# Sums over tokens with both signs of phi in one weight: 65 moving columns for 129, and due times by refinement

## The chip, the cores and the metric

The kernel runs on one core of a Trainium2 chip. The metric is the device time of one execution in microseconds; lower is better. Eight runs of the kernel before gave a median of 390.5 us, between 389.41 and 391.68. All profile numbers come from one profiled execution of it.

The engines are TensorE (PE in the profile; its weight loads are PEld), VectorE (DVE), ScalarE (ACT), GpSimd (POOL) and the SyncE queue (SP), which issues nearly all DMA transfers. Each runs its own queue of instructions in order and waits on semaphores for the others.

## The reference

The input is 2048 tokens of 512 features, in bf16. Two layers follow one another, each of a linear attention with 32 heads of 16 features (Hedgehog) and a gated MLP of 1376 hidden features. Cut to what matters:

```python
pq = einsum("bhsd,hdf->bhsf", q, w_phi);  pk = einsum("bhsd,hdf->bhsf", k, w_phi)
phi_q = concatenate([softmax(pq), softmax(-pq)], -1)       # 32 features per head
phi_k = concatenate([softmax(pk), softmax(-pk)], -1)
kv  = einsum("bhsf,bhsd->bhfd", phi_k, v)                  # sum over all tokens
z   = einsum("bhsf->bhf", phi_k)                           # sum over all tokens
o   = einsum("bhqf,bhfd->bhqd", phi_q, kv) / (einsum("bhqf,bhf->bhq", phi_q, z)[..., None] + 1e-6)
x = x + o @ wo                                             # of layernorm(x)
x = x + ((relu(g) * u) @ W_down)                           # g, u = layernorm(x) @ W_gate, W_up
```

For every head a 32 x 17 table is needed: 16 positive and 16 negative features of the keys, times 16 value features and a one for z. Only blocks of equal head are wanted; a matmul over 128 keys' features and 128 value features also computes the products of unequal heads.

## The kernel before

**Tiles.** The 2048 tokens are 16 tiles of 128. A layer has these stages per tile:

- *Norm and keys.* Statistics and normalisation on DVE (L610, L611, L621, two small ACT steps L616 and L618), a transpose by DMA (`turn`, L598, tile `xnTA`), four matmuls of 512 columns for the key features (L641; `w_phi` is folded into the weight beforehand) and four for the values (L647). ACT takes exp of the keys with both signs into `ek` (L644), DVE sums 16 features at a time (L652), ACT makes the reciprocal by log and exp (L655, L657), and `phi` (L661) multiplies, on DVE or POOL, half a tile in an instruction, into `phiK`. The values are copied from PSUM to `vext`, which has one extra column of ones.
- *Sums over tokens* (`kvz`, L675 to L686). Eight matmuls per tile: one for each block b of eight heads and each sign s, weight `ph[:, s, b*128:(b+1)*128]` (128 tokens x 128 features), moving `vext` of 129 columns (128 value features and the ones). They add up over all 16 tiles of a layer in three PSUM banks of pool `q`: groups 0 to 2, 3 to 5, 6 and 7.
- *R* (`Keys.build`, L688). When the last sum is in, DVE multiplies each bank by the head mask `Mf` into the bf16 tile `R`, laid out as [128 features, 8 groups, 18, 8 heads]: 16 value features, z, and a column of the mask itself (written once, L551). The masked products are zeros where heads differ, so all of R is written each time.
- *Queries* (L715, exp with both signs on ACT into `Eq`, L719), per chunk of four tiles.
- *Attention* (`attend`, L725). For each tile eight matmuls of 144 columns (`erq`, L733) with `Eq` as weight and a group of R as moving operand, in three PSUM buffers of pool `q` (3, 3 and 2 matmuls). Each buffer is emptied by two copies through `evac`: the numerators into `N`, the denominators into `DS`. Then DVE makes `m`, `den`, `rden`, `w`, `pr` and `o` (L749 to L761), `o` is transposed (by DMA, or by TensorE and a copy for the first two tiles), projected (L765) and added to X (L769).
- *MLP* (`mlp`, L774) in blocks of 1, 1, 2, 4, 4, 2, 2 tiles (the second layer ends in 1, 1): statistics and centring on DVE, transpose, gate and up matmuls (L829; the last 96 hidden features apart, L805), relu on ACT (L833), a copy of the up projection by `evac`, their product on DVE (L837), down matmuls (L862) and the residual (L869). In layer 0 each tile goes on to the norm and keys of layer 1.

**PSUM.** Eight banks: three in pool `q` (sums, erq), five in pool `b` (everything else), L459.

**The order of the work.** The program is not written in its final order. Each operation is an `Op` with an engine, a cost, a due time, the operations it depends on and the buffers that it takes and uses. `plan` (L76) is a list scheduler: at each step it picks, on the engine that can start first, the ready operation with the lowest due time, by costs written into the file (`mm`, `act`, `dve` and so on), and emits it. The instructions of each engine run in the order so found. Before, the due times come from `DUE`, a table of 2112 stored numbers, one per operation, which replaces the due times given in the code (`arrange`, L160). A second stored table, `PLACE` (301 characters, 117 of them "1"), decides for every copy out of PSUM and every phi product whether it stays on the engine that the code names first or changes to its other one: ACT or DVE for copies, POOL or DVE for phi. By default copies go to ACT (the code names DVE for some of the first ones), and phi follows `PHI0` in layer 0 and is DVE for most of layer 1.

**Idle fillers.** Until the first sum, matmuls of zeros (L557) fill gaps of TensorE.

Of the kernel before, what the change touches and what calls it, by code (L numbers as in the profile page):

```python
# [8 lines left out]
P = 128  # L9
# [10 lines left out]
GV = P + 1  # L20
# [139 lines left out]
def arrange(ops):  # L160
# [8 lines left out]
    assert len(ops) == len(DUE)  # L169
    for n, o in enumerate(ops):  # L170
        o.n, o.due = n, DUE[n]
        o.follow += {taker[b] for b in o.uses} - set(o.deps) - set(o.follow)
        for d in o.deps:
            d.then.append(o)
        for d in o.follow:
            d.behind.append(o)
    return plan(ops)
# [26 lines left out]
DVE0 = (85, 170)  # L204
STATS = (592, 692)
# [11 lines left out]
class K:  # L217
# [8 lines left out]
PLACE = (  # L226
    "0000010000001001000100000001010000000000101100111000110100010000100001001000000000100100101011010000"
    "1000000000111101000110100111010010111011010100100110101011010000101011001110000110000000111000000101"
    "1100101010101000101000110000000100000100110010110011011101000010011110010100010111101011111011011010"
    "1"  # L230
)
# [3 lines left out]

DUE = (
    7238437, 6462738, 6444986, 6386567, 5992333, 6335033, 6406961, 6303369, 5712831, 6413612, 6092682, 6414331,
    7434675, 6620170, 4674366, 7071562, 5773774, 7071571, 7071548, 7071565, 5376048, 6430379, 5994524, 5038937,  # L240
    5154841, 6509440, 6825368, 6847621, 6377520, 5995707, 6404704, 6443663, 6844264, 5995988, 6959386, 6784947,
    6825065, 6420713, 6382495, 5410283, 6400005, 6216969, 7068818, 6425562, 6371338, 6325356, 5116853, 6509939,
    6325403, 6399345, 6420906, 6420903, 6403761, 5854885, 5527927, 6112383, 6040357, 6246638, 6429204, 6120059,
    6425464, 5996011, 5410344, 5937857, 5997209, 6629949, 6159020, 5837281, 6159017, 5812166, 6376057, 6112054,
    5527770, 5778741, 5859984, 6246016, 5780700, 6191478, 5995462, 6415371, 6420993, 5937862, 6218721, 6366108,
    6398876, 6355933, 6040362, 6353076, 6692318, 6246832, 6301941, 6333817, 6305472, 6420324, 6246635, 6282608,
    6010072, 6010132, 5937718, 5517502, 5527720, 5962872, 6417645, 6375834, 6115594, 6417622, 6376951, 6040201,
    6418805, 6367897, 6418065, 6246853, 6246635, 6280551, 6416172, 6413450, 5812833, 5734989, 5527730, 6415701,
    6589688, 6660152, 6259055, 6293340, 6418857, 6193613, 6400771, 6242577, 5594853, 5897821, 6418101, 6246214,
    6414310, 6418410, 6417781, 6293326, 6418213, 6337803, 6493628, 5823924, 6281803, 6385607, 6385616, 6414319,  # L250
    6392870, 6399165, 6376822, 6423098, 6382355, 6246148, 6189671, 6413294, 5970487, 6354744, 6354741, 6148511,
    6557117, 6415725, 7222162, 6412246, 6420372, 6418246, 6414304, 6330448, 6400107, 6407313, 6121354, 6246632,
    6247421, 6281496, 6418264, 6416104, 6292977, 6417603, 6446115, 6428567, 5823973, 6417942, 6323224, 6435617,
    6413175, 6372016, 6395620, 6424638, 6323105, 6245911, 6245802, 6350052, 6399800, 6339292, 6104846, 6199296,
    6400901, 6500288, 6429150, 6504253, 6415373, 5944333, 5942659, 6414885, 6419661, 6437686, 6424884, 6421739,
# [163 lines left out]
def kernel(  # L419
# [209 lines left out]
    class Keys:  # L629
# [57 lines left out]

        def build(self, due):  # L688
            made = []
            for k in range(3):  # L690
                ng = 3 if k < 2 else 2

                def num(k=k, ng=ng):
# [278 lines left out]
```

The softmax here doesn't subtract the row's maximum and nothing guards it: scores larger than these inputs give would overflow.

## Time and profile before

| | |
|---|---|
| time, median of 8 runs | 390.5 us |
| time of the profiled execution | 390.68 us |
| its span, first to last instruction | 388.9 us |
| granted TensorE clock | 1.00 |
| TensorE busy | 381.6 us (98%) |
| VectorE busy | 309.2 us (80%) |
| ScalarE busy | 217.7 us (56%) |
| GpSimd busy | 43.5 us (11%) |
| sums: 256 matmuls of 129 columns (L678) | 19.4 us busy |
| erq: 256 matmuls of 144 columns (L733) | 26.8 us busy |
| copies of the up projection | 46 on ACT (26.1 us), 37 on DVE (25.1 us) |
| phi products | 39 on POOL (42.8 us), 25 on DVE (16.7 us) |
| copies of N: ACT / DVE | 63 / 33 |
| value copies: ACT / DVE | 21 / 11 |

A group's row has its line, engine, operation, tiles and count, then busy time, the mean duration of one in ns, and the idle time of the engine just before. Matmuls are pipelined: a matmul of 129 columns lasts 220 ns from start to end, but the next one starts long before that end, so busy time of a run of matmuls is much less than count times duration, and a short gap between matmuls can hide in the duration of the one before. A wait's row reads: who waited, for whom, us in all, times, longest. A window's row gives busy time and count of each engine, then clock, DMA share and GB/s.

### The profile page before, as it was taken

How to read it: one execution, taken by the hardware profiler on the slowest of the kernel's cores; microseconds unless marked ns; L12 is line 12 of the kernel's file. 1: busy time of each engine (PE TensorE's matmuls, PEld its weight loads, DVE VectorE, ACT ScalarE, POOL GpSimd, SP SyncE). 2: the span in 40 equal slices, each digit the busy share in tenths (PEclk: the TensorE clock that was granted, in tenths of full speed). 3: DMA queues.
4: the chain of work that ended last, by engine and by line, in shares of the span. 5: the costliest groups of instructions: out<-in, count | busy, mean ns of one | idle time of the engine just before them, and what ended most of it. 6: DMA issues, size and time to landing. Idle time of an engine off the chain costs nothing.

```text
span 388.9 us, 7655 instructions
## 1 busy us (share of the span) xinstructions
PE 381.6 (98%) x2833; PEld 231.6 (60%) x2833; DVE 309.2 (80%) x785; ACT 217.7 (56%) x569; POOL 43.5 (11%) x45
## 2 busy tenths in 40 slices
PE   8999998999999999999999999999999999999996
PEld 4544565967654554454767655578765545547674
DVE  6999988999999985479767486799998999455243
ACT  6999979744556545134665668976425520443111
POOL 0344630000200400012220122000000000000000
DMA  8479840122322221102201000023233122201110
GB/s 247 103 165 196 189 136 1 37 55 50 78 59 42 56 53 30 27 16 54 43 0 15 14 15 0 2 33 64 56 70 81 37 50 66 54 7 29 56 35 29
DMA packets 60871, 22.84 MB, mean 59 GB/s; under 512 B 52673, under 2 KB 59809, under 8 KB 60833
## 3 DMA queue, kind: packets, MB, share of 16 engines
q1 hardware_dynamic: 60416, 21.95, 26.2%
q8 instruction: 22, 0.36, 0.4%
q10 hardware_dynamic: 416, 0.39, 0.3%
q14 instruction: 17, 0.13, 0.1%
HBM read 7.91 MB, written 2.10 MB: 26 GB/s over the span
## 4 chain that ended last, share of the span: by engine, by line
PE 82%; DVE 7%; ACT 5%; DMA 3%; issue 1%; DVEq 0%; ACTq 0%
PE b L829 34%; PE b L862 19%; PE b L765 6%; PE b L641 5%; PE b L647 5%; PE b L715 4%; PE q L678 3%; PE b L805 3%; PE q L733 2%; ACT Eq L719 2%; DMA xnTA<-xn 2%; ACT ek L644 1%; DMA xnTB<-xn 1%; DVE pr L758 1%; DVE X L769 1%; DVE bstB L610 1%
## 5 line engine op out<-in xcount | busy, mean ns | idle before, releaser
L829 PE MATMUL b<-xnTB,wgu 128*128 128x128 bf16 (+2 forms) x1200 | 150.8, 279 | 0.0
L829 PEld LDWEIGHTS <-wgu 128*128 128x128 bf16 x1200 | 97.8, 98 | 42.8
L862 PE MATMUL b<-wd,hT 128*128 128x512 bf16 (+2 forms) x363 | 83.4, 373 | 0.0
L833 ACT ACTIVATE gu<-b 128x512 bf16<-128x512 f32 (+1 forms) x83 | 48.1, 582 | 48.2 <-PE b L829 45.4
L661 POOL TENSOR_TENSOR phiK<-ek,sk 128x512 bf16<-128x512 bf16 x39 | 42.8, 1116 | 193.5 <-ACT sk L657 144.7
L862 PEld LDWEIGHTS <-hT 128*128 128x128 bf16 (+1 forms) x363 | 34.8, 98 | 34.9 <-DVE hT L837 0.3
L837 DVE TENSOR_TENSOR hT<-gu 128x512 bf16<-128x512 bf16 (+1 forms) x83 | 33.7, 407 | 18.5 <-ACT gu L563 16.9
L644 ACT ACTIVATE ek<-b 128x512 bf16<-128x512 f32 x64 | 35.9, 598 | 17.1 <-PE b L641 17.0
L652 DVE TENSOR_REDUCE sk<-ek 128x64 f32<-128x1024 bf16 x32 | 38.6, 1209 | 8.1 <-ACT ek L644 8.0
L563 ACT CAST gu<-b 128x512 bf16<-128x512 f32 (+1 forms) x46 | 26.1, 566 | 31.7 <-PE b L829 31.7
L719 ACT ACTIVATE Eq<-b 128x512 bf16<-128x512 f32 x64 | 35.3, 623 | 4.7 <-PE b L715 4.5
L564 DVE CAST gu<-b 128x512 bf16<-128x512 f32 (+1 forms) x37 | 25.1, 677 | 13.2 <-PE b L829 13.0
L869 DVE SCALAR_TENSOR_TENSOR X<-b,rsB,X 128x512 bf16<-128x512 f32 (+1 forms) x33 | 23.4, 726 | 15.1 <-PE b L862 15.0
L641 PE MATMUL b<-Wk,xnTA 128*128 128x512 bf16 x128 | 32.9, 379 | 0.5 <-DMA xnTA<-xn 0.5
L647 PE MATMUL b<-wv,xnTA 128*128 128x512 bf16 x128 | 32.4, 379 | 0.6 <-DMA xnTA<-xn 0.6
L563 ACT CAST N<-q 128x384 bf16<-128x384 f32 (+1 forms) x63 | 28.0, 461 | 8.3 <-DVE pr L758 3.2
L765 PE MATMUL b<-wo,oT 128*128 128x512 bf16 x128 | 32.5, 379 | 0.0
L715 PE MATMUL b<-xnTA,Wq 128*128 128x512 bf16 x128 | 31.2, 379 | 0.0
L733 PE MATMUL q<-R,Eq 128*128 128x144 bf16 x256 | 26.8, 226 | 1.0 <-ACT N L563 0.5
L733 PEld LDWEIGHTS <-Eq 128*128 128x128 bf16 x256 | 19.9, 98 | 11.3 <-issue 1.4
L610 DVE BATCH_NORM_STATS2 bstA<-X 128x6 f32<-128x512 bf16 x32 | 21.2, 682 | 3.0 <-DMA X<-in_A_x_dram 2.9
L769 DVE TENSOR_TENSOR X<-X,b 128x512 bf16<-128x512 bf16 x32 | 21.6, 677 | 1.6 <-PE b L765 1.5
(71 smaller groups left out, 397.3 us busy)
## 6 DMA issues: line engine op xcount, KB each, us to landing
out_dram<-X SPq DMA_DIRECT2D x15, 128.0 KB, 1.7
X<-in_A_x_dram SPq DMA_DIRECT2D x6, 256.0 KB, 3.3
wgu<-in_B_W_gate_dram SPq DMA_DIRECT2D x4, 344.0 KB, 4.3
wgu<-in_B_W_up_dram SPq DMA_DIRECT2D x4, 344.0 KB, 5.2
wd<-in_B_W_down_dram SPq DMA_DIRECT2D x5, 256.0 KB, 4.8
wv<-in_A_wqkv_dram SPq DMA_DIRECT2D x2, 256.0 KB, 4.2
wo<-in_A_wo_dram SPq DMA_DIRECT2D x4, 128.0 KB, 3.6
oT<-o SPq DMA_TRANSPOSE x28, 2.4
```

What stands on the lines that cost most here:

```text
L563: both = {"ACT": ("ACT", act(cols), lambda: nc.scalar.copy(out=out_(), in_=in_()), False), "DVE": ("DVE", dve(cols), lambda: nc.vector.ten ...
L641: k = op("PE", mm(4, 512), due, lambda: [nc.tensor.matmul(kp.t[:], lhsT=xnTA[c][:, b, cols], rhs=Wk2[:, b, :], start=(b == 0), stop=(b == ...
L644: e = [op("ACT", act(512), due, lambda s=s: nc.scalar.activation(out=ek.t[:, s, :], in_=kp.t[:], func=AF.Exp, scale=1.0 - 2.0 * s), [k], [ ...
L647: v = op("PE", mm(4, 512), due_v, lambda: [nc.tensor.matmul(vp.t[:], lhsT=xnTA[c][:, b, cols], rhs=wv[:, b, :], start=(b == 0), stop=(b == ...
L661: e.tensor_tensor(out=ph.t[:].rearrange("p s (h f) -> p (s h) f", f=DH)[:, lo:lo + n], in0=ek.t[:].rearrange("p s (h f) -> p (s h) f", f=D ...
L715: q = op("PE", mm(4, 512), due(c, b), lambda b=b, qp=qp: [nc.tensor.matmul(qp.t[:], lhsT=Wq2[:, m, b * P:(b + 1) * P], rhs=xnTA[c][:, m, : ...
L719: done.append(op("ACT", act(512), due(c, b), lambda b=b, s=s, qp=qp: nc.scalar.activation(out=Eq[c][:, b, s, :], in_=qp.t[:], func=AF.Exp, ...
L733: pe.append(op("PE", mm(len(groups), GE), due, lambda ps=ps, groups=groups: [nc.tensor.matmul(ps.t[:, n * GE:(n + 1) * GE], lhsT=Eq[c][:, ...
L765: a = op("PE", mm(4, 512), due + 3, lambda: [nc.tensor.matmul(yp.t[:], lhsT=oT.t[:, b, :], rhs=wo[:, b, :], start=(b == 0), stop=(b == NB ...
L829: nc.tensor.matmul(ps.t[:, q * W:(q + 1) * W], lhsT=wgu[:, s, b, g * P:(g + 1) * P], rhs=xT.t[:, b, 0:W], start=(b == 0), stop=(b == NB - 1))
L833: nc.scalar.activation(out=gu.t[:, 0, 0:cols], in_=gp.t[:, 0:cols], func=AF.Relu)
L862: nc.tensor.matmul(yp.t[:, 0:c1 - c0], lhsT=h.t[:m, f * W + i * P:f * W + (i + 1) * P], rhs=wd[:m, f, c0:c1], start=(f == 0), stop=(f == N ...
```

## The change

Four things change together.

1. *The sums.* `ek` and `phiK` are laid out as [8 groups of four heads, 2 signs, 64 features]. A group's weight is its four heads with both signs, again 128 columns; the moving operand is the values of these four heads and a one, 65 columns (`vext` is laid out as 8 groups of 65, padded to 66). There are still eight matmuls per tile. The eight results of 65 columns fit in two banks: even groups in one, odd ones in the other. The planner books 8 x 40 ns for them (`SUMS`).
2. *R.* A result now has the positive features of its four heads in partitions 0 to 63 and the negative ones in 64 to 127. `erq` is unchanged, so R keeps its layout, and `build` moves halves between partitions: for each bank and sign one masked product over 64 partitions x 256 elements and one for z, eight pairs in all over two layers for six. The parts of R that are never written are zeroed once at the start (`c_r0`).
3. *PSUM.* Pool `q` has two banks for three, pool `b` six for five. `erq` uses pool `q` too: the three buffers of a tile now take turns in two banks.
4. *The order.* `DUE` goes. The due times given in the code are refined: `plan` runs, `back` goes through the plan from its end and gives each operation the latest time at which it could end in a reversed schedule as its due time, and this is repeated ten times; the due times of the plan with the earliest end are kept. `PLACE` is empty, so every copy and every phi product stays on the engine that the code names.

The diff, without the stored tables:

```diff
-GV = P + 1
+NG = 2 * NB
+HG = HB // 2
+GQ = P // 2
+GV = GQ + 1
...
+def back(ops):
+    left = {o: len(o.then) + len(o.behind) for o in ops}
+    ready = dict.fromkeys(ops, 0.0)
+    clock = dict.fromkeys(HOP, 0.0)
+    open_ = {e: [o for o in ops if o.eng == e and not left[o]] for e in HOP}
+    for _ in ops:
+        best = None
+        for e, cand in open_.items():
+            if cand:
+                at = [(max(clock[e], ready[o] + o.end - o.start - o.spent), o) for o in cand]
+                first = min(t for t, o in at)
+                if best is None or first < best[0]:
+                    best = first, max((o for t, o in at if t <= first + 1), key=lambda o: (o.start, o.n))
+        t, o = best
+        clock[o.eng] = t + o.spent
+        o.due = -clock[o.eng]
...
-def arrange(ops):
+def refine(ops, rounds):
...
-    assert len(ops) == len(DUE)
     for n, o in enumerate(ops):
-        o.n, o.due = n, DUE[n]
+        o.n = n
...
+    best = None
+    for k in range(rounds):
+        dues = [o.due for o in ops]
+        span = max(o.end for o in plan(ops))
+        if best is None or span < best[0]:
+            best = span, dues
+        back(ops)
+    for o, due in zip(ops, best[1]):
+        o.due = due
     return plan(ops)
...
+SUMS = (8 * 40, 8 * 40 + 170)
...
-PLACE = (
...
+ROUNDS = 10
+PLACE = ""
...
-    p_q, p_b = psum("q", 3), psum("b", 5)
+    p_q, p_b = psum("q", 2), psum("b", 6)
-    p_ek, p_phi = pool("ek", 4, [2, D]), pool("phiK", 4, [2, D])
+    p_ek, p_phi = pool("ek", 4, [NG, 2, GQ]), pool("phiK", 4, [NG, 2, GQ])
-    p_v = pool("vext", 5, [NB, GV])
+    p_v = pool("vext", 5, [NG, GV + 1])
...
+    c_r0 = op("DVE", dve(1152, 4), 15000, lambda: nc.vector.memset(R[:], 0.0), follow=[c_z], name="R0", port=True)
...
-                out=ek.t[:, s, :], in_=kp.t[:], func=AF.Exp, scale=1.0 - 2.0 * s), [k], [ek] if s == 0 else [],
+                out=ek.t[:, :, s, :], in_=kp.t[:].rearrange("p (g e) -> p g e", e=GQ), func=AF.Exp, scale=1.0 - 2.0 * s), [k], [ek] if s == 0 else [],
...
             def kvz():
-                for g in range(2 * NB):
-                    b, s = g // 2, g % 2
-                    nc.tensor.matmul(self.bufs[g // 3].t[:, (g % 3) * GV:(g % 3 + 1) * GV],
-                                     lhsT=ph.t[:, s, b * P:(b + 1) * P], rhs=vx.t[:, b, :],
-                                     start=(self.n == 0 and g % 3 == 0), stop=(self.n == T - 1),
+                for g in range(NG):
+                    b, k = g // 2, g % 2
+                    nc.tensor.matmul(self.bufs[k].t[:, b * GV:(b + 1) * GV],
+                                     lhsT=ph.t[:, g, :, :].rearrange("p s e -> p (s e)"), rhs=vx.t[:, g, 0:GV],
+                                     start=(self.n == 0 and b == 0), stop=(self.n == T - 1),
                                      skip_group_check=True)
...
-            z = op("PE", mm(8, GV), due_z, kvz, a + [v] + (self.before if first else self.sums[:1]),
+            z = op("PE", SUMS, due_z, kvz, a + [v] + (self.before if first else self.sums[:1]),
...
+            for k in range(2):
+                for s in range(2):
+                    rows, to = slice(s * GQ, (s + 1) * GQ), slice(k * GQ, (k + 1) * GQ)
+                    heads, mask = slice(k * HG, (k + 1) * HG), slice(s * HG, (s + 1) * HG)
+                    def src(k=k, rows=rows):
+                        return self.bufs[k].t[rows, 0:NB * GV].rearrange("p (g e) -> p g e", e=GV)
+                    def num(src=src, s=s, rows=rows, to=to, heads=heads, mask=mask):
+                        nc.vector.tensor_tensor(
+                            out=R[to, s::2, 0:DH, heads],
+                            in0=src()[:, :, 0:GQ].rearrange("p g (j d) -> p g d j", d=DH),
+                            in1=Mf[rows, mask].unsqueeze(1).unsqueeze(1).to_broadcast([GQ, NB, DH, HG]), op=Alu.mult)
...
-    order = arrange(ops)
+    order = refine(ops, ROUNDS)
```

## The prediction

> **What bounds the kernel now.** I read the page first, then the waits, then windows of equal length, then the instructions in order of time around the sums and around the first attention tiles. The page: TensorE is busy for 381.6 of 388.9 us and carries 82% of the chain that ended last.
>
> ```profile
> span 388.9 us, 7655 instructions
> PE 381.6 (98%) x2833; PEld 231.6 (60%) x2833; DVE 309.2 (80%) x785; ACT 217.7 (56%) x569; POOL 43.5 (11%) x45
> PE 82%; DVE 7%; ACT 5%; DMA 3%; issue 1%; DVEq 0%; ACTq 0%
> L678 PE MATMUL q<-vext,phiK 128*128 128x129 bf16 x256 | 19.4, 220 | 0.0
> ```
>
> Of the 7.3 us that TensorE is not busy, 1.3 lie before its first matmul and 3.1 after its last, so under 3 us are left inside. All that TensorE waited for, after the zeros of the start:
>
> ```profile
> PE b L647 <- DMA xnTA<-xn: 0.6, 1, 0.6
> PE b L641 <- DMA xnTA<-xn: 0.5, 1, 0.5
> PE q L733 <- ACT N L563: 0.5, 1, 0.5
> PE q L733 <- DVE DS L564: 0.4, 1, 0.4
> ```
>
> The windows (columns: PE, weight loads, DVE, ACT, POOL busy) show who stands behind TensorE in each stage:
>
> ```profile
> 14.00:47.00 33.00, 31.91 (x201) 16.47 (x199) 30.96 (x57) 31.85 (x98) 16.13 (x16) 1.00 0.86 178
> 60.00:80.00 20.00, 18.93 (x248) 15.35 (x247) 19.15 (x61) 16.33 (x49) 0.00 (x0) 1.00 0.13 25
> 100.00:120.00 20.00, 20.00 (x139) 12.06 (x138) 19.93 (x66) 11.50 (x37) 2.07 (x2) 1.00 0.30 60
> 240.00:260.00 20.00, 19.81 (x198) 13.35 (x197) 16.37 (x53) 19.15 (x53) 0.00 (x0) 1.00 0.05 10
> ```
>
> In the first stage (14 to 47, keys and sums of layer 0) ACT and DVE are as full as TensorE; in 60:80 and 240:260, where attention opens, ACT is nearly full and TensorE idles 1.07 and 0.19 us; in 100:120 DVE is full and TensorE loses nothing. Single instructions give the paces:
>
> ```profile
> 54.34 2.01 PE L678 MATMUL q<-vext,phiK 128*128 128x129 bf16 x32
> 375.44 4.63 PE L829 MATMUL b<-xnTB,wgu 128*128 128x128 bf16 x80
> 53.68 2.06 ACT L719 ACTIVATE Eq<-b 128x512 bf16<-128x512 f32 x4 [0.29 <-PE b L715]
> 65.65 0.35 PE L733 MATMUL q<-R,Eq 128*128 128x144 bf16 x3
> 65.93 0.89 ACT L563 CAST N<-q 128x384 bf16<-128x384 f32 x2
> 66.49 0.83 PE L733 MATMUL q<-R,Eq 128*128 128x144 bf16 x6 [0.49 <-ACT N L563]
> 29.22 5.90 DMA xnTA<-xn
> ```
>
> A run of n matmuls lasts n-1 paces and one matmul's 0.22 us, so the 129-column matmul of the sums comes every (2.01-0.22)/31 = 57.7 ns, a 128-column one every 55.8. An ACT copy of 512 columns comes every (2.06-0.60)/3 = 0.49 us, one of 384 every 0.89-0.49 = 0.40. The last lines are one bank wait (erq stands until ACT has copied its bank) and the slowest transpose, from issue to landing.
>
> **The change, part by part.**
>
> *The sums.* 256 matmuls of 129 columns become 256 of 65; their weights stay 128x128. From 512 columns (0.216 us: the chain has runs of 8 in 1.73) to 129 the pace falls by 0.41 ns per column; if that holds, 65 columns take 31 ns and 256 x 26.5 = 6.8 us go. No matmul of the trace is under 128 columns, so the other end is the pace of the smallest rows, 55.8: 0.5 us goes. A weight load still precedes every matmul, and nothing shows loads closer together than 55 ns in a steady run, so the straight line is not safe; the line is the nearer evidence, and I take 40 ns, nearer to it: 256 x 17.5 = -4.5 us. The Trainium skill ("TensorE: Matmul & The Clock Gate", "LDWEIGHTS" and "Weight-path perf modes") speaks against this: a load takes its columns at 1.2 per ns, 107 ns for 128, and the fast load about halves that. The 55.8 ns row already excludes 107; by the halved figure, about 53 ns as an estimate, the sums would save some 1.2 us and my time would be 3.3 us later.
>
> *Where half of that saving falls.* 16 of the 32 tiles' sums are layer 0's, in the stage where ACT has 31.85 of 33 us. ACT does no less there; three value copies move to it (vext, 3 x 0.49 = 1.5 us), since PLACE is empty and layer 0's DVE copies were three. So 2.2 us of TensorE's gain can turn into waiting, plus 1.5 us: between 0 and +3.7; TensorE's queue can fill with Q matmuls whose copies come later, so I take +1.2.
>
> *Placement elsewhere.* In all of the program ACT gets the 37 up-projection copies and the 33 pairs of N and DS copies that DVE had, and 10 of its 11 value copies; DVE gets 16 of POOL's 39 phi products. By paces ACT gains 37 x 0.49 + 33 x about 0.47 + 10 x 0.49, some 38 us of work; DVE loses about as much. Where DVE was full (100:120) TensorE was not idle, so this relief is worth nothing; cover for it is MLP matmuls. Where ACT was full, the move costs.
>
> *Opening of attention, layer 0.* The built order of the changed program has, on TensorE, eight erq groups (3,3,2,3,3,2,3,3 matmuls) with nothing between them, then the first turn and projection. With two banks the eighth needs six groups copied out, all by ACT: four of 0.40+0.10 (N, DS) and two of about 0.30+0.10, 2.8 us, starting 0.35 after the first matmul; the seven groups before it are 19 matmuls of 62 ns, 1.2 us. So 3.25-1.2 = 2.0 us are lost there. TensorE runs its queue in order, so all that stands behind waits with it. The projection then waits for tile 0: three groups copied at 1.9 us, its DVE steps m, den, rden, w, pr, o (0.21+0.18+0.34+0.21+0.68+0.41 = 2.0), the turn 0.4 and ACT's copy 0.62 make 4.9 us, against 1.6 us of queued matmuls: 3.3 lost in all. Before the first MLP matmuls another chain of 2.9 us (residual, statistics, centring, turn, copy) stands over 2.4 us of work: 0.6 with the hand-offs. That is 3.9. Before, the same opening loses 1.07 us by the window, and as each of some six gaps hides about 0.16 us of a matmul's drain, 2.0 from start to start. Extra: +1.9; bounds 0 (the gap of before) and +4 (if Eq copies queue among them).
>
> *Opening, layer 1.* From the last sums to the second projection the order puts 11.8 us on TensorE (32 Q, 32 erq, 16 sums, 8 turns, 8 projections) and on ACT 16 Eq, 8 large and 3 small N, 11 DS and 2 oT copies, 7.8+3.2+0.9+1.1+1.0 = 14.0: 2.2 behind, and the first MLP matmuls follow their ACT copy at once, 0.6. Before lost 0.19 plus drains, about 0.8. Extra +2.0; bounds 0 and +4.
>
> *R.* Eight pairs of half-height products for six pairs: per layer 4 x 0.33 + 4 x 0.09 = 1.7 us on DVE (paces of the 256-column row) for 1.5. The order keeps three Q groups, 2.6 us, between the last sum and the first erq, which hides it; were the 64-row form twice as slow, 1 us per layer would show. The memset of R, about 0.55 us by the 0.27 of the zero tile half its size, lies before DVE's first input lands. 0, bound +2.
>
> *Transposes and loads.* Between issue of a transpose in layer 0 and its consumer the order leaves 3.6 to 6.2 us of matmuls, median 4.1, where before had 3.7 to 6.3, median 5.0; landings there took 2.4 to 5.9. SP's queue carries the same loads between them, moved past some. +0.6, bounds 0 and +2. The first keys lose 0.3 in the same way (an xn turned for three tiles in a row). At the end, eight half-width down matmuls (0.87 us) cover the last products where before seven full ones did: 0.
>
> Sum against the profiled execution's 390.68 us: -4.5 +1.2 +1.9 +2.0 +0.6 +0.3 = +1.5, so 392.2. That execution is 0.2 above the median of 390.5, which leaves the forecast at about 392.
>
> **The rivals.**
> 1. *The waits are covered after all, faster.* One mechanism: TensorE's queue is filled better than my counting by hand says at the two openings. If they cost no more than before, +3.9 goes and the time is 388.1; it is faster than before by 0.2% as soon as the extra idle in all (6.0 in my sum) is under 3.7 us at 40 ns, or under 6.0 at 31. For it: before, DVE and ACT stood at 19.9 and 19.15 of 20 and TensorE still lost almost nothing. Against: eleven erq groups follow the last user of their bank by under 0.5 us, where before had two, and both of those waited.
> 2. *Weight loads set the pace, slower.* At 55.8 ns only 0.5 us goes: 396. For it: a load per matmul, steady loads never under 55 ns apart. Against: the straight line down to 128 columns.
> 3. *The order loses more than the openings.* Ten rounds of refinement replace 2112 stored due times; if the first stage pays its whole 3.7, transposes 2 and the openings their upper ends 8, the time is 390.7-4.5+14 = 400. Against: elsewhere I found no place in the order where a matmul stands too near its producer.
>
> **How the numbers follow.** Forecast, 391.3 to 395: 0.42. Rival 1, 387 to 389.7: 0.26. Within 0.2% (0.8 us, about what can be told here from no change), the sum's small change: 0.13. Rival 2, 395 to 397: 0.10. Rival 3, 397 to 404: 0.09. Slower 0.42+0.10+0.09 = 0.61, same 0.13, faster 0.26. Range: all costs at their low ends with 31 ns would be 384, all at their high ones 404; leaving out about 1 in 10 on each side gives 387 to 400.
>
> **What the profile after would show.** The sums' row with 65 columns and a run of 8 lasting 0.22+7 paces: 0.50 us at 40 ns, 0.44 at 31, 0.61 at 55.8. TensorE waiting at erq for N and DS, at the projection for oT, 3 to 5 us together. ACT busy near 265, DVE near 268, POOL near 26 us. TensorE's idle outside 50 to 75 and 240 to 260 us under 3 us; more there means rival 3. R ending before the first erq. Wrong would make me a pace under 31 or over 55 ns, or waits on transposes of over 2 us.

## The result, and the profile after

The changed kernel takes 393.09 us (median of 11 runs, 392.49 to 394.6) beside 390.64 for the kernel before (32 runs): a ratio of 1.0069, interval 1.0058 to 1.0080. It is slower by 0.7%, 1.1 us more than forecast. (The record lists a twelfth execution, of 391.45 us, that is not in the median; with it the median is 393.08.) Its profiled execution took 392.57 us with a span of 390.5; the kernel before's took 390.68 with 388.9.

From the page of the changed kernel: span, busy time, the granted clock in 40 slices and the chain that ended last; and, from its groups by line, the row of the sums.

```profile
span 390.5 us, 7700 instructions
PE 378.6 (97%) x2832; PEld 226.2 (58%) x2832; DVE 277.4 (71%) x692; ACT 256.0 (66%) x683; POOL 26.5 (7%) x29
...
PEclk9999998999999999999999999999999999999999
...
PE 73%; ACT 14%; DVE 9%; issue 2%; DMA 1%; POOL 1%; DVEq 0%; ACTq 0%
...
L537 PE MATMUL q<-vext,phiK 128*128 128x65 bf16 x256 | 13.7, 194 | 1.6 <-DVE phiK L520 1.1 <-POOL phiK L520 0.3
```

The sums are busy 13.7 us (19.4 before). TensorE is busy 3.0 us less in all and the span is 1.6 us longer, so it stands still more. ACT's share of the chain rose from 5% to 14%. The seventh clock slice is no longer a 9, which nothing in the prediction had foreseen. The waits of TensorE that bear on the argument (who, for whom, us, times, longest; left out are the wait for the zeros of the start and, but for the last row, those of 0.4 us and less):

```profile
PE b L628 <- ACT oT L422: 1.3, 2, 0.7
PE q L537 <- DVE phiK L520: 1.1, 2, 0.7
PE q L596 <- ACT DS L422: 1.1, 2, 0.6
PE b L668 <- ACT xnTB L422: 0.9, 2, 0.7
PE q L596 <- ACT N L422: 0.8, 4, 0.3
PE q L537 <- POOL phiK L520: 0.3, 1, 0.3
```

Before, the four longest waits after the zeros of the start came to 2.0 us. Now erq (L596), the projection (L628) and the first gate matmuls (L668) stand behind ACT's copies, and the sums (L537) behind phi. The same four windows as before, with the columns PE, weight loads, DVE, ACT, POOL, clock, DMA share and GB/s:

```profile
14.00:47.00 33.00, 31.85 (x206) 15.07 (x205) 32.92 (x56) 31.45 (x98) 17.72 (x16) 1.00 0.71 175
60.00:80.00 20.00, 17.80 (x188) 12.88 (x186) 18.05 (x63) 16.98 (x60) 0.00 (x0) 0.91 0.14 27
100.00:120.00 20.00, 20.00 (x162) 13.39 (x160) 20.00 (x57) 12.23 (x38) 0.00 (x0) 1.00 0.34 64
240.00:260.00 20.00, 17.50 (x180) 11.87 (x181) 14.54 (x52) 19.74 (x62) 0.00 (x0) 1.00 0.05 10
```

TensorE loses 2.20 us in 60:80 (1.07 before) and 2.50 in 240:260 (0.19 before), and ACT is full in the latter. In 60:80 the mean clock is 0.91.

To see where the time went I add up, stage by stage, the time from start to start and compare it with the work: every matmul at the pace of an undisturbed run, columns / 2.4 + 2.5 ns (the straight line through 215.8 for 512 columns and 55.8 for 128, which the runs of the trace before show), 65 columns at 32.5 (eight sums at 55.96 below, the next instruction at 56.22). The difference is "lost".

| stage | before: elapsed, lost | after: elapsed, lost | lost more | predicted |
|---|---|---|---|---|
| first matmul to first sum | 16.69, 3.19 | 16.60, 3.32 | +0.13 | +0.3 |
| sums of layer 0 | 38.11, 1.61 | 38.39, 2.32 | +0.71 | +1.2 |
| last sum to first erq (R) | 2.65, 0 | 2.62, 0 | 0 | 0 |
| first erq to first gate matmul, layer 0 | 9.67, 2.06 | 10.66, 5.89 | +3.83 | +1.9 |
| to the first sum of layer 1 | 60.81, 0.15 | 45.79, 0.22 | +0.07 | +0.6 in all |
| sums of layer 1 | 111.53, 0.30 | 126.32, 1.06 | +0.76 | |
| last sum to first erq (R) | 2.65, 0 | 2.62, 0 | 0 | 0 |
| first erq to first gate matmul, layer 1 | 9.38, 0.64 | 11.08, 3.04 | +2.40 | +2.0 |
| from there to the last matmul | 132.68, 0.48 | 131.84, 0.67 | +0.19 | |

Work falls from 375.8 to 369.5 us, 6.3 less: 256 x (56.3 - 32.5) = 6.1 from the sums and one filler matmul of 0.2. Lost time rises by 8.1; the first matmul starts 0.15 earlier. 8.1 - 6.3 - 0.15 = +1.65, the difference of the spans. One row needs care: the opening of layer 0 loses 3.8 us more but takes only 1.0 us longer, since 2.8 us less of work stand in it (4.77 us for 7.61).

Three details, in order of time on TensorE. A run of eight sums lasts 0.42 us; its matmuls last 191 to 204 ns each, median 193. So the pace is (0.42 - 0.19) / 7 = 32.9 ns. Here is the opening of layer 0 (start, us, then who, and the idle time before it):

```profile
55.96 0.42 PE L537 MATMUL q<-vext,phiK 128*128 128x65 bf16 x8
56.22 2.75 PE L578 MATMUL b<-xnTA,Wq 128*128 128x512 bf16 x12
58.80 0.54 PE L596 MATMUL q<-R,Eq 128*128 128x144 bf16 x6
59.82 0.28 PE L596 MATMUL q<-R,Eq 128*128 128x144 bf16 x2 [0.48 <-ACT DS L422]
60.31 0.71 PE L596 MATMUL q<-R,Eq 128*128 128x144 bf16 x6 [0.20 <-ACT N L422]
61.65 0.28 PE L596 MATMUL q<-R,Eq 128*128 128x144 bf16 x2 [0.63 <-ACT DS L422]
62.14 0.71 PE L596 MATMUL q<-R,Eq 128*128 128x144 bf16 x6 [0.20 <-ACT N L422]
62.79 0.40 PE L460 MATMUL b<-ident,o 128*128 128x128 bf16 x4
63.87 1.89 PE L628 MATMUL b<-wo,oT 128*128 128x512 bf16 x4 [0.69 <-ACT oT L422]
...
67.11 1.04 PE L628 MATMUL b<-wo,oT 128*128 128x512 bf16 x4
```

In the kernel before, twelve matmuls of Q (L715, 2.6 us) stand between the first erq groups (L733):

```profile
58.78 0.66 PE L733 MATMUL q<-R,Eq 128*128 128x144 bf16 x8
59.28 1.03 PE L715 MATMUL b<-xnTA,Wq 128*128 128x512 bf16 x4
60.33 1.03 PE L715 MATMUL b<-xnTA,Wq 128*128 128x512 bf16 x4
61.69 1.03 PE L715 MATMUL b<-xnTA,Wq 128*128 128x512 bf16 x4
64.00 1.04 PE L765 MATMUL b<-wo,oT 128*128 128x512 bf16 x4
```

In the new order no Q matmul is left in this stretch, so they do not cover its waits. The first projection starts some 5 us after the first erq in both (5.2 and 5.1). No run puts the Q matmuls back, so what their place costs by itself is not shown.

The projection at 63.87 takes 1.89 us where the next takes 1.04. The windows of 2 us over this stretch show why:

```profile
58.00:60.00 2.00, 1.52 (x13) 0.90 (x12) 0.48 (x2) 2.00 (x7) 0.00 (x0) 1.00 0.00 0
60.00:62.00 2.00, 1.09 (x10) 0.60 (x8) 1.41 (x5) 2.00 (x9) 0.00 (x0) 1.00 0.00 0
62.00:64.00 2.00, 1.16 (x11) 0.73 (x11) 1.76 (x7) 2.00 (x9) 0.00 (x0) 0.90 0.00 0
64.00:66.00 2.00, 2.00 (x8) 0.90 (x8) 1.16 (x3) 0.91 (x3) 0.00 (x0) 0.50 0.00 0
66.00:68.00 2.00, 2.00 (x16) 1.28 (x14) 2.00 (x9) 1.96 (x7) 0.00 (x0) 0.74 0.02 4
```

After some 4 us with TensorE busy a little over half the time, the granted clock is 0.50 from about 63.5 to 67 us. Which of the waits comes from what, and whether the waits cause the fall of the clock, the two traces can't say; the runs below were made for that.

### The profile page after: what moved, and what is told of

Same layout as the page of the kernel before. It is cut to its first block, busy times and chain, and to the rows that moved or that the text cites. A ratio compares the mean times of both kernels' runs of the same rounds, so it can differ in the third digit from the quotient of the medians.

```text
span 390.5 us, 7700 instructions
## 1 busy us (share of the span) xinstructions
PE 378.6 (97%) x2832; PEld 226.2 (58%) x2832; DVE 277.4 (71%) x692; ACT 256.0 (66%) x683; POOL 26.5 (7%) x29
## 4 chain that ended last, share of the span: by engine, by line
PE 73%; ACT 14%; DVE 9%; issue 2%; DMA 1%; POOL 1%; DVEq 0%; ACTq 0%
PE b L692 32%; PE b L725 18%; PE b L628 5%; ACT ek L503 4%; ACT Eq L582 4%; PE b L500 3%; PE b L578 3%; PE b L506 3%; PE b L668 2%; PE q L596 2%; ACT vext L422 2%; DVE X L632 1%; DVE bstB L469 1%; PE q L416 1%; PE q L537 1%
## 5 line engine op out<-in xcount | busy, mean ns | idle before, releaser
L692 PE MATMUL b<-xnTB,wgu 128*128 128x128 bf16 (+2 forms) x1200 | 147.5, 279 | 0.0
L422 ACT CAST gu<-b 128x512 bf16<-128x512 f32 (+1 forms) x83 | 47.8, 575 | 26.9 <-PE b L692 26.6
L422 ACT CAST N<-q 128x384 bf16<-128x384 f32 (+1 forms) x96 | 45.2, 477 | 5.9 <-PE q L596 4.4
L520 POOL TENSOR_TENSOR phiK<-ek,sk 128x512 bf16<-128x512 bf16 x23 | 25.8, 1142 | 210.9 <-ACT sk L516 200.9
L628 PE MATMUL b<-wo,oT 128*128 128x512 bf16 x128 | 33.8, 387 | 1.8 <-ACT oT L422 1.3
L520 DVE TENSOR_TENSOR phiK<-ek,sk 128x512 bf16<-128x512 bf16 x41 | 30.6, 782 | 0.0
L596 PE MATMUL q<-R,Eq 128*128 128x144 bf16 x256 | 27.4, 229 | 2.0 <-ACT DS L422 1.1
L596 PEld LDWEIGHTS <-Eq 128*128 128x128 bf16 x256 | 20.1, 99 | 10.6 <-issue 3.3
L621 DVE TENSOR_TENSOR pr<-N,w 128x1024 bf16<-128x1024 bf16 x32 | 21.9, 686 | 1.2 <-DVE w L618 0.5
## 6 DMA issues: line engine op xcount, KB each, us to landing
X<-in_A_x_dram SPq DMA_DIRECT2D x6, 256.0 KB, 3.1
wd<-in_B_W_down_dram SPq DMA_DIRECT2D x5, 256.0 KB, 5.1
wv<-in_A_wqkv_dram SPq DMA_DIRECT2D x2, 256.0 KB, 4.2
```

The lines of the kernel that those rows point to most:

```text
L422: both = {"ACT": ("ACT", act(cols), lambda: nc.scalar.copy(out=out_(), in_=in_()), False), "DVE": ("DVE", dve(cols), lambda: nc.vector.ten ...
L520: e.tensor_tensor(out=ph.t[:].rearrange("p g s (h f) -> p (g s h) f", f=DH)[:, lo:lo + n], in0=ek.t[:].rearrange("p g s (h f) -> p (g s h) ...
L596: pe.append(op("PE", mm(len(groups), GE), due, lambda ps=ps, groups=groups: [nc.tensor.matmul(ps.t[:, n * GE:(n + 1) * GE], lhsT=Eq[c][:, ...
L628: a = op("PE", mm(4, 512), due + 3, lambda: [nc.tensor.matmul(yp.t[:], lhsT=oT.t[:, b, :], rhs=wo[:, b, :], start=(b == 0), stop=(b == NB ...
L692: nc.tensor.matmul(ps.t[:, q * W:(q + 1) * W], lhsT=wgu[:, s, b, g * P:(g + 1) * P], rhs=xT.t[:, b, 0:W], start=(b == 0), stop=(b == NB - 1))
```

## The experiments

The theory at the start: the sums give what a straight line through the paces says, about 6 us, and the new order (refined due times, empty placement) takes it back and more, above all in the two openings, where ACT copies everything. The rivals: the two banks in place of three for erq are what costs; weight loads keep most of the gain from appearing; the fall of the clock is what costs.

**The sums under the order of before.** The changed sums, R and `ek`/`phiK`/`vext` layouts, with the stored due times and placement, and three buffers taken in pool `q` as before (the sums use two of them). The planner books the old costs, so that each engine has the order that it had before. Cut to its main lines, against the changed kernel:

```diff
-    p_q, p_b = psum("q", 2), psum("b", 6)
+    p_q, p_b = psum("q", 3), psum("b", 5)
...
-            self.bufs = [Buf(p_q) for _ in range(2)]
+            self.bufs = [Buf(p_q) for _ in range(3)]
...
-    order = refine(ops, ROUNDS)
+    order = arrange(ops)
```

> The new sums and the new R under the order of the kernel before: stored due times, stored placement, three banks in pool q (a tile's sums use two of them), five in pool b, and the planner books the old costs, so that every engine has its old order; only the 65-column sums, the zeroing of R and the fourth pair of R products differ. Theory (the sums are a gain by themselves, the order costs): the sums give 256 x 25 ns = 6.4 us less of TensorE; in layer 0 ACT and DVE are as full as TensorE, so part of its 3.2 us stays; 384 to 387 us. Rival (the gain is given back to the engines behind TensorE, whatever the order): 389 to 391 us, with TensorE waiting for phi before the sums.

Measured: 386.34 us (385.83 to 387.89), ratio 0.9887, interval 0.9864 to 0.9910. It is 1.1% faster than the kernel before, 6.7 us faster than the changed one, and the fastest of all versions here. From its order of time:

```profile
43.70 0.42 PE L692 MATMUL q<-vext,phiK 128*128 128x65 bf16 x8
```

The pace is the same 32.9 ns. The stretch from the first to the last sum of layer 0 falls from 38.11 to 36.32 us and that of layer 1 from 111.53 to 108.93: 1.8 and 2.6 of the some 3.1 that each half of the sums gives up. The openings stay at 9.64 and 9.38 (9.67 and 9.38 before). So the sums are worth 4.3 us where nothing else moves, and in layer 0 more than a third of the gain turns into waiting. ACT and DVE are as full there as TensorE (31.84, 31.65 and 31.17 of the 33 us from 14 to 47), but the waits that the trace shows in these sums are for transposes by DMA (1.6 us, 1.1 before) and for phi of DVE (0.3, none before).

**The order without the sums.** The kernel before, sums and three banks kept, with due times refined in ten rounds and an empty placement.

```diff
-    order = arrange(ops)
+    order = refine(ops, 10)
...
-PLACE = (
...
+PLACE = ""
```

> The kernel before with its old sums, old R and three banks, but due times by ten rounds of refinement and the default placement. Theory (order and placement alone cost about 8 us): 396 to 400 us, lost around the first attention tiles of both layers. Rival (the two banks are what costs, since erq finds a bank less): close to before, 390 to 393 us.

Measured: 395.23 us (394.62 to 395.42), ratio 1.0108, interval 1.0090 to 1.0125. This lies between the two forecasts. The order and the placement cost 4.6 us by themselves, and without any fall of the clock: all six executions show 0.999 or 1.00. Nor is it lost in both openings, as the theory had it: the opening of layer 0 takes 9.75 us (9.67 before), the one of layer 1 11.22 (9.38 before), and the stretch before the first sum is 1.0 us longer. The new sums are worth only 395.23 - 393.09 = 2.1 us on top of this order (1.5 by the two ratios), half or less of what they are worth in the stored order.

**Placement and due times.** The stored placement beside refined due times, first with the old sums:

```diff
-    order = arrange(ops)
+    order = refine(ops, 10)
```

> The kernel before with one thing changed: its due times come from ten rounds of refinement instead of the stored list; the sums, the three banks and the stored placement stay. With the same edit and an empty placement it took 395.2 us, 4.6 more than before. Theory 'the stored placement belongs to the stored order, and is worth nothing, or less than nothing, beside refined due times': 396 to 401 us, since with the new sums the stored placement beside refined due times took 398.4, 5.2 more than the empty one. Rival 'the empty placement is what costs the 4.6 us (ACT as the only copier in the openings)': 390 to 393 us.

Measured: 402.69 us (401.87 to 403.1), ratio 1.0301, interval 1.0282 to 1.0320; a little over the range of the first theory, and far from that of the rival. The same placement in the changed kernel:

```diff
-PLACE = ""
+PLACE = (
...
```

> The changed kernel with the stored placement (117 of 301 copies and products on their other engine) and refined due times. Theory (the empty placement is what the openings lose by): 389 to 392 us. Rival (due times, not placement: a placement searched for another order does not fit a refined one): 394 us or more, waits spread over the middle and the end.

Measured: 398.37 us (4 runs), ratio 1.0192, interval 1.0169 to 1.0215. That is the rival's time, though not its place: against the changed kernel, the sums of layer 0 take 2.8 us longer and the two openings 1.8 and 1.5. Together (medians in us, ratios to the kernel before):

| | stored due times, stored placement | refined, empty | refined, stored placement |
|---|---|---|---|
| 129 columns, three banks | 390.64 | 395.23 (1.0108) | 402.69 (1.0301) |
| 65 columns (three banks in the first column, two in the others) | 386.34 (0.9887) | 393.09 (1.0069) | 398.37 (1.0192) |

Stored due times beside an empty placement were not tried. Beside refined due times the empty placement is not what costs: it is 5 to 7.5 us better than the stored one. The stored placement is worth something only beside its own due times, and against that pair the refined order with the empty placement costs 4.6 us with the old sums and 6.8 with the new ones.

**The banks.** The changed kernel with three banks in pool `q` and five in `b`:

```diff
-    p_q, p_b = psum("q", 2), psum("b", 6)
+    p_q, p_b = psum("q", 3), psum("b", 5)
```

> The changed kernel with three banks in pool q and five in pool b, refined anew. Theory (ACT's copies set the openings, not the banks): no gain, 392 to 395 us. Rival (the bank waits of erq cost the 6 us): 388 to 390 us, with no wait of erq for N or DS.

Measured: 394.17 us (393.36 to 394.89), ratio 1.0085, interval 1.0064 to 1.0106: not faster than with two banks. The refinement finds another order for it. In its profile the two openings are shorter (10.06 and 10.13 us, lost 4.67 and 1.60), but the 40 gate matmuls after the second one lose 1.74 where they lost 0.01, and the sums of layer 1 lose 1.55. The first opening is no fair comparison: the profiled execution kept its clock at 1.00, the changed kernel's did not, and four of the six executions with three banks show a mean clock of 0.995 or 0.996. TensorE still waits for N and DS at erq (1.3 and 0.6 us), with three banks too. The third bank moves the waits; its lack is not the cause of the 2.5 us. Beside the old sums in three banks (395.23) it also gives the new sums' worth in a refined order with the banks alike: 1.1 us.

**The openings filled, and five banks for the rest.** One bank less in pool `b`, and in a second kernel that bank used for 93 matmuls of zeros wherever the planner expects TensorE to wait after the first erq.

```diff
-    p_q, p_b = psum("q", 2), psum("b", 6)
+    p_q, p_b = psum("q", 2), psum("b", 5)
+    p_f = psum("f", 1)
...
+                opened = opened or o.name == "erq"
+                if opened and o.name != "kvz":
+                    fill(max(0, int((o.start - free - 60) / 56)))
```

> The changed kernel with five banks in pool b instead of six, nothing else; control for e7. Theory: 393 to 396 us, the same waits at both openings, and a clock below 1.00 between 60 and 80 us. Rival (the sixth bank matters): over 396 us.

> The changed kernel with five banks in pool b, the eighth bank taking matmuls of zeros (128 columns, 93 in all) that fill TensorE's planned gaps from the first attention tile on; e8 is the same without them. Theory (the clock drops because TensorE stands still at the opening of layer 0, which costs some 1.6 us): granted clock 1.00 in every slice and 1 to 2 us less than e8. Rival (the clock is chance, or fillers do not count): as e8 within 0.5 us, or slower by what the fillers delay (up to 5 us of them).

Measured: 392.74 us (391.74 to 393.62) without the fillers, ratio 1.0051, interval 1.0035 to 1.0067; 392.79 (391.67 to 393.49) with them, ratio 1.0048, interval 1.0032 to 1.0065. The sixth bank of pool `b` is worth nothing. The control was expected at 393 to 396 us with a fall of the clock; neither came. The fillers only take the place of waiting: the first opening takes 10.35 us in both. They could not settle the clock, since it stays at 1.00 in both profiles: with five banks the refined order puts more matmuls into that opening (at least 7.15 us of work, by the records, where the changed kernel has 4.77).

**The changed kernel again.**

> The changed kernel as it is, once more, beside the next three on the same chip. Theory (the clock drops after the opening of layer 0 whenever TensorE stands still there for so long): the granted clock is again below 1.00 between 60 and 70 us. Rival (chance): 1.00 throughout, and the execution up to 1.6 us shorter than the first profiled one, 391 us.

Measured: 393.28 us (392.2 to 394.63), ratio 1.0066, interval 1.0041 to 1.0092, and a second profile, of an execution of 394.59 us. The clock falls in it too, for longer (0.50 from about 63 to 70 us):

```profile
62.00:64.00 2.00, 1.42 (x12) 0.88 (x11) 1.79 (x6) 2.00 (x8) 0.00 (x0) 0.83 0.00 0
64.00:66.00 2.00, 1.32 (x4) 0.43 (x4) 1.53 (x4) 1.71 (x6) 0.00 (x0) 0.50 0.00 0
66.00:68.00 2.00, 2.00 (x14) 1.45 (x12) 1.29 (x3) 1.05 (x4) 0.00 (x0) 0.50 0.00 0
68.00:70.00 2.00, 2.00 (x8) 0.89 (x8) 1.04 (x8) 0.93 (x4) 0.00 (x0) 0.50 0.02 4
```

The opening takes 11.84 us and loses 7.06, 1.2 more than in the first profile. The record has the mean clock of every execution. Of 18 of this kernel (12 and 6) three show 1.00 (391.45, 392.2 and 393.64 us, mean 392.4), eleven 0.996 (mean 393.2) and four 0.991 (mean 394.2). So the fall comes in most executions, not in all; in the two profiles it lasts 3.4 us (mean clock 0.996) and 6.8 us (0.991). Within each of the three groups the times still spread by 1.7 to 2.2 us, and the 16 executions of the kernel before beside the run in the stored order, all at 0.999 or 1.00, by 3.1: most of the spread is not the clock.

**Copies on DVE in the openings.** The changed kernel in its own order, but N and DS of the second erq group of the first four tiles of each layer are copied by DVE at the same place.

```diff
+                                 "Q on DVE" if t < 4 and k == 1 else "Q",
...
-            o.emit()
+            if o.name == "Q on DVE":
+                o.alt[2]()
+            else:
+                o.emit()
```

> The changed kernel in its own order, with one thing moved: for the first four attention tiles of each layer the copies of the second erq group (N and DS) run on DVE at the same place of the order, 16 copies for each layer's 24 staying on ACT. Theory (ACT as the only copier costs the openings): about 2 us less than the changed kernel, 391 us; TensorE's time from the first erq to the first MLP matmul shorter by 1 us or more in each layer. Rival (two banks cost them, whoever copies): the same as the changed kernel within 0.5 us.

Measured: 394.64 us (393.93 to 395.41), ratio 1.0096, interval 1.0073 to 1.0118: 1.4 us slower than the changed kernel in the same set. The openings take 11.46 and 11.99 us. Relief for ACT is no gain by itself: these copies now stand on DVE among `m` to `o`, on whose end the turn and the projection wait. DVE reaches the second N behind `pr` of the first tile, erq waits for it, and the first projection comes 5.72 us after the first erq (5.07 before this edit):

```profile
63.30 0.54 PE L596 MATMUL q<-R,Eq 128*128 128x144 bf16 x6 [0.97 <-DVE N L423]
```

That ACT copies alone is thus not shown to be the cause of the longer openings; that ACT and DVE form one chain there is what the order of time shows.

**The clock.** The changed kernel in its own order; each of the first eight erq groups of layer 0 is computed twice, into the same bank.

```diff
             o.emit()
+            erqs += o.name == "erq"
+            if o.name == "erq" and erqs <= 8:
+                o.emit()
```

> The changed kernel in its own order, with one thing added: each of the first eight erq groups of layer 0 is computed twice in a row into the same bank (22 matmuls more, 1.4 us of TensorE work, in a stretch in which TensorE stands still for some 2.9 us between 58.8 and 64 us). Theory 'the granted clock fell because TensorE was only about half busy for some 4 us, and the halved clock costs about 1.6 us behind it': TensorE is then about 80% busy in that stretch, the granted clock stays at 1.00 in 64 to 68 us, the projection's matmuls come every 0.22 us and not 0.43, and from the first erq to the first gate matmul it takes 9.2 to 10.2 us and not the 10.7 to 11.8 of the two profiles of the changed kernel: 391 to 392.5 us. Rival 'the fall of the clock has another cause, such as time since the start or what the other engines do': the clock falls again in 62 to 70 us, the opening takes 11 us or more, and the time is 393 to 395, since each repeat also keeps the copy of its bank back by 0.19 us. In layer 1 nothing is changed: its opening should take 11.1 us as before.

Measured: 391.79 us (391.36 to 392.2), ratio 1.0026, interval 1.0016 to 1.0035. With 1.4 us more work on TensorE the kernel is 1.3 us faster than without (1.5 against its second set of runs), and the intervals do not overlap. Its opening, in order of time, and in windows of 2 us:

```profile
59.16 0.91 PE L596 MATMUL q<-R,Eq 128*128 128x144 bf16 x12
60.37 1.49 PE L596 MATMUL q<-R,Eq 128*128 128x144 bf16 x16 [0.29 <-ACT DS L422]
62.30 1.50 PE L596 MATMUL q<-R,Eq 128*128 128x144 bf16 x16 [0.44 <-ACT DS L422]
63.63 0.39 PE L460 MATMUL b<-ident,o 128*128 128x128 bf16 x4
64.70 1.04 PE L628 MATMUL b<-wo,oT 128*128 128x512 bf16 x4 [0.68 <-ACT oT L422]
...
66.90 1.04 PE L628 MATMUL b<-wo,oT 128*128 128x512 bf16 x4
...
68.67 0.35 PE L596 MATMUL q<-R,Eq 128*128 128x144 bf16 x3 [0.19 <-ACT N L422]
69.27 0.50 PE L668 MATMUL b<-wgu,xnTB 128*128 128x192 bf16 x4 [0.25 <-ACT xnTB L422]
```

```profile
59.00:61.00 2.00, 1.63 (x21) 1.26 (x20) 0.00 (x0) 1.86 (x8) 0.00 (x0) 1.00 0.00 0
61.00:63.00 2.00, 1.48 (x20) 1.16 (x19) 1.73 (x6) 1.99 (x8) 0.00 (x0) 1.00 0.00 0
63.00:65.00 2.00, 1.32 (x18) 0.97 (x16) 1.79 (x6) 2.00 (x7) 0.00 (x0) 1.00 0.00 0
65.00:67.00 2.00, 1.74 (x17) 1.04 (x16) 1.84 (x5) 1.84 (x6) 0.00 (x0) 1.00 0.00 0
```

TensorE is 66 to 87% busy here, the clock stays at 1.00 and the projection takes 1.04 us. The repeats hold the projection back by 0.47 us (5.54 after the first erq, against 5.07), and from the projection to the first gate matmul it is 4.57 us against 5.60 and, in the second profile, 6.57. Layer 1 is untouched, and its opening takes 11.08 us in both. All eleven executions show a mean clock of 0.999 or 1.00, where 15 of 18 without the repeats show less. So TensorE's half-busy stretch brings the fall, and the fall costs 1.0 us behind it in the first profile and 2.0 in the second; the means of the executions by their clock (0.7 and 1.8 us over those at 1.00) agree. In the whole time 1.3 of the 2.5 us by which the changed kernel is slower go with it, the price of the repeats included; at full clock, 391.79 is still 0.26% over the kernel before.

Two reservations. The kernel with copies on DVE, whose clock falls in four of six executions, is no slower in those (394.4 to 395.0 us) than in the two at 1.00 (393.9 and 395.4). And the repeats ran on another chip than the second set of the changed kernel (for the first set the record names no chip). Against the chip as the cause speaks that the kernel before keeps 0.999 to 1.00 on that set's chip too, and so does what the last section works out for the profiles of that chip.

## Why the prediction was right, and where its terms were not

The forecast, slower by waits at the two openings that with the smaller terms outweigh the sums, is what happened; the sum of +1.5 us against the profiled execution stands beside +1.9. But the nearness of the total hides terms that were off by 2 us and cancelled, and is luck in part.

- *The sums.* Mis-sized: 40 ns a matmul and -4.5 us; measured 32.9 ns and -6.1 (-6.3 from the prediction's own 57.7 ns for the old row). The straight line (31) was nearly right, and hedging it toward the smallest row was the error. The prediction's estimate of about 53 ns, by the load times in the Trainium skill ("TensorE: Matmul & The Clock Gate", "LDWEIGHTS" and "Weight-path perf modes"), does not hold as a pace: every one of the 256 matmuls has its own load, recorded with 95 to 101 ns, and they still follow one another in 32.9 ns. The section "Wait — 56ns, not 53.3ns?" of the same page gives columns / 2.4 + 2.5 ns, an estimate of 29.6 for 65 columns, much nearer. The run of eight (0.42 us) is below all three lengths of the list of signs, since a matmul of 65 columns lasts 0.19 us and not the 0.22 put in there.
- *Layer 0's sums.* +1.2 predicted, +0.7 measured, but by another engine than named. The term was worked out from ACT, with three value copies more; ACT has 31.45 us of the 33 and not more than the 31.85 before, with three queries' exps less in that window (13 for 16). The waits are for `phiK` of DVE (0.4 us; DVE has 32.92 of 33, 30.96 before) and POOL (0.3). DVE is fuller partly because its phi products became dearer: 41 with a mean of 782 ns, where 25 had 694. Five of the nine that overlap one of POOL's last 1.43 to 1.55 us; the other four and the 32 that overlap none last 0.66 to 0.69. In the order before, the eight that overlapped lasted 0.68 to 0.71, but for one with 0.91. This the prediction had at nothing, and it is 4.1 us of the 9 by which DVE is over its 268.
- *Opening of layer 0.* The total of 3.9 us lost was 2.0 too small. The chain to the first projection was worked out as 4.9 us against 1.6 of work, 3.3 lost; it is 5.07 (58.80 to 63.87), 3.5 lost. The second part, from there to the gate matmuls, was put at 0.6 and lost 2.4. Of this 1.0 is the clock, by the difference to the kernel with repeats, and 1.4 remain. In that kernel's lines, at the paces above, these are 0.6 before the second projection (66.90), 0.4 before the erq at 68.67, which waits for ACT's copy of N, and 0.4 before the first gate matmuls, which wait for ACT's copy of `xnTB`. So two steps fell short: the chain was costed at full clock (1.0), and 0.8 of waits behind ACT's copies were not counted. The +4 end of the range held it.
- *Opening of layer 1.* +2.0 predicted, +2.4 measured; the waits are for ACT's copies of oT, N and `xnTB` and for `o` of DVE. No fall of the clock there (1.00 in 240:260), though TensorE loses 2.5 us: between 248 and 254 us it is busy 4.5 of 6.
- *Transposes, loads, first keys.* +0.9 predicted; the stages that hold them lost 0.4 more in all, and the waits on transposes are 0.2 and 0.3 us. Too dear.
- *Sums of layer 1.* Not in the sum at all; +0.76. Twelve sums before the end of the layer TensorE waits 0.7 us for phi of DVE. Two pairs of phi products stand before it on DVE: the first, beside two of POOL's, takes 2.91 us, the second, alone, 1.28:

```profile
235.44 1.06 POOL L520 TENSOR_TENSOR phiK<-ek,sk 128x512 bf16<-128x512 bf16 x1 [182.20 <-ACT sk L516]
235.59 2.91 DVE L520 TENSOR_TENSOR phiK<-ek,sk 128x512 bf16<-128x512 bf16 x2
239.03 1.28 DVE L520 TENSOR_TENSOR phiK<-ek,sk 128x512 bf16<-128x512 bf16 x2
240.37 0.30 PE L537 MATMUL q<-vext,phiK 128*128 128x65 bf16 x4 [0.72 <-DVE phiK L520]
```

  Had the first pair taken 1.3 us too, the second would have been ready before it was wanted; this is worked out from the rows and was not run.
- *R.* Right: hidden behind the three Q groups (2.62 us from the last sum to the first erq, nothing lost). A product over 64 partitions lasts 0.42 us. The end of the program costs nothing, as said.
- *Signs in the profile.* TensorE waits 3.5 us for N, DS and oT (3 to 5 foretold). Outside 50 to 75 and 240 to 260 us its idle time is 11.9 - 2.8 - 2.5 - 1.2 (before the first matmul) - 3.1 (after the last) = 2.3 us (under 3). POOL 26.5 is as said. ACT's 256.0 is what the working gives (217.7 + 38), and the 265 written in the list of signs was a slip; DVE's 277.4 is 9 over the 268 there.
- *Rivals.* The first (waits covered) fell: the openings lost 6.2 us more. The second (weight loads set the pace) fell with 32.9 ns. The third (the order loses elsewhere) fell for the changed kernel, as outside the openings and layer 0's sums 1.2 us more are lost. But its root, that the refined order is worth less than the stored one, is what all the runs agree on.

Left open: which part of the 4.6 us is the due times and which the placement, and what would shorten the openings for good: a third bank moved the waits elsewhere, and copies on DVE and fillers did not shorten them.

## What to carry to other kernels

A gain on the busiest engine must be priced together with the order in which it is placed: here the same edit of the sums was worth 4.3 us in an order that was left alone and 1 to 2 in one planned anew, and planning anew cost 4.6 by itself. Change the work inside a stored order first, and replace the order in a separate step. Where a new order leaves TensorE half busy for some 4 us, look at the granted clock behind that stretch, and fill the waits with repeated matmuls if it falls: 1.4 us of useless work bought 1.3 us.

## What was not expected of the hardware

- *Loads at 33 ns.* The weight loads of the sums are recorded with 95 to 101 ns each, yet matmuls with a load each follow one another in 32.9 ns, so that several loads must overlap. From the query for the sums' line (duration min/median/max, first and last start):

```profile
L537 PEld LDWEIGHTS <-phiK x256: 95/98/101, 17.6 to 241.6; 128*128 128x128 bf16 x128
L537 PE MATMUL q<-vext,phiK x256: 191/193/204, 17.8 to 241.6; 128*128 128x65 bf16 x128
```

- *Phi products on VectorE and GpSimd, side by side.* Of two that overlap, the one that starts second can last much longer. DVE's at 235.59, begun just behind POOL's (235.44, 1.06 us), lasts 1.45 us where one alone lasts 0.68. At 51.6 it is the other way round: DVE's starts first and lasts 0.68, and POOL's (51.69) lasts 1.55 for some 1.06. So the order decides whether the engine nearer to the critical path pays.

- *The clock falls without a long gap, and in steps of 3.41 us.* No single wait of TensorE in this opening is over 0.7 us, and the clock still fell to 0.50. The traces hold the granted clock as stretches of time, and each stretch that they hold whole lasts a multiple of 3.41 us: in the first profile 58.03 (17 times), 3.41 at half clock and 324.27 (95 times); in the second 6.83 at half clock (twice); 3.41 in the two other profiles with a fall, those with copies on DVE and with the stored placement. If these steps are laid over TensorE's work, each matmul at its pace, the four steps that end in a fall hold 0.74 to 1.10 us of work (22 to 32%). Before the last matmul, no step at full clock that a fall does not follow holds less than 1.35 (40%, in the kernel with old sums, refined due times and stored placement). The kernel with repeats has 1.75 or more in every step. So the limit lies between 1.10 and 1.35 us of work in such a step, as far as these profiles tell. On the chip of the second set a step with 1.58 (the kernel with three banks) brought no fall either, so the repeats would be expected to keep the clock there as well. Where the steps lie against the program differs from profile to profile; that this decides which executions of one kernel fall is likely, but was not shown. The Trainium skill ("TensorE: Matmul & The Clock Gate", "A second HAM failure mode: psum-queue depth-cycling") tells of this in another kernel, with matmuls of 512 columns: it goes round its PSUM banks, pauses briefly between groups of matmuls, and the clock goes down and up again. Here erq goes round two banks, and the clock does so in most executions. The same page's "HAM oscillation — how this bites in real kernels" asks only that no gap be longer than about 3.4 us; by that rule nothing would have fallen here.
